# The output gradient's load, the place of the rows' tiles, and the time of b2's sums in a backward kernel

## The chip, the cores and the metric

The program runs on one NeuronCore of a Trainium2 chip. Its engines work beside each other: TensorE (PE in the profile, its weight loads PEld), VectorE (DVE), ScalarE (ACT), GpSimd (POOL) and SyncE (SP), which issues most of the transfers. Each engine works through its own list of instructions in order and waits on semaphores for the others. The metric is the device time of one launch in microseconds (us); lower is better.

## What is computed

One layer, forward and backward, for a sequence of 2048 rows of 512 elements: a spectral filter (FFT over both axes, a product with a complex filter, inverse FFT) and a feed-forward block with a squared ReLU, both modulated by a condition `c`. All gradients are returned.

```python
mod = (_silu(c) @ w_mod).reshape(c.shape[0], 6, 1, -1)
sa, ca, ga, sb, cb, gb = ...
h = _layernorm(x) * (1 + ca) + sa
x = x + ga * irfft2(rfft2(h) * (w_r + 1j * w_i))
h = _layernorm(x) * (1 + cb) + sb
x = x + gb * (relu(h @ w1 + b1) ** 2 @ w2 + b2)
_out, _vjp = jax.vjp(f, A_x, A_w_r, A_w_i, B_w1, B_b1, B_w2, B_b2, c, w_mod)
_grads = _vjp(grad_out)
```

The outputs that matter here: `out_2`, `out_3` (the filter's gradient, w_r and w_i), `out_4`, `out_5` (w1, b1), `out_6`, `out_7` (w2, b2), `out_9` (w_mod), `out_1` (A_x) and `out_8` (c). `grad_out` is the output gradient.

## The kernel before

The function named `tile_adaLN_...` is one long program that a framework orders: tiles are taken from pools, pools lie on two stacks in SBUF (a left one and a right one, `side="right"`), and a pool that is released gives its place to later ones. An instruction that writes a tile waits for all that used the earlier tiles at that place. The framework also draws up each engine's list by priority, and `tc.issue_after(x)` puts what is issued inside it behind x on the same engine. SP's transfers share eight semaphores in turn, so a transfer waits until the eighth before it has landed.

The change lies in the last third, from line 1058 on. What happens there, in order:

- **Spectral stage, backward** (`spec_f23` with `ew_b` and `after_b`, groups gi = 0 to 7). For each group, TensorE makes G (L323, L311), VectorE makes the product Z and the filter's gradient gW from it (`cmul`, L418 to L421), and SP writes gW to `out_2` and `out_3` (L1168). `after_b` fills in TensorE work: products of w1's gradient (`grad_w1`, L1124, sixteen in all; two halves make one tile gw1, which POOL writes, L1130), b1's sums (`grad_b1`, with the tile b4), and four of the six blocks of the modulation's gradient (`gm.emit`, tiles wmc, gmbc, gm_junk and gwm; after groups 0, 1, 3 and 4). It also loads the matrix LG (1.5 MB, after group 4 in the program's text, L1174) and the first two columns hn of the hidden activations, by a transposing load (`load_hn`, L1067).
- **G1** (`spec_g1`, L346 to L367): 128 small matmuls of Z with LG, and casts of their results.
- **Rows stage** (`row_pair`, eight pairs of row tiles): TensorE does psT (L375) and psY (L385); ScalarE and VectorE the layer norm's gradient on two tiles n1 and gxl that SP loads (`load_rows3`, L1216 and L1217). VectorE reads n1 first at L1275. Column sums follow on TensorE (L1256) with a lag of two pairs.
- **w2's gradient** (`grad_w2`, fourteen products of sixteen matmuls, L1196) fills TensorE between the pairs and after them. Each product reads the whole output gradient g_sb (16 tiles of 512 columns, 2 MB) and one hn. VectorE scales the result into gw (L1199), SP writes it (L1200). Products take turns in two PSUM buffers named mm.
- **b2's sums** (`grad_b2`, after the pair t = 10): sixteen matmuls into four quadrants (L1207); `add_quadrants` copies them as b4 (ScalarE, L1097) and the rest as b4l (VectorE, L1098); later, `add` sums the quadrants by two matmuls (L1103), also in a buffer mm, and writes the row. `add` is put on a list that `run_later` empties after the next product of w2's gradient.
- **End**: the other two blocks of the modulation's gradient, the rest of the products, and c's gradient (L1312 to L1320).

The pools in question. Left stack, upwards: gwa (G, gw1 four times, b4), lg2 (LG), spb (Z), f23b (Xb), ewb (p1, p2, gW). Right stack, downwards: lf2 (four spectral matrices LFb), gmp (wmc, gmbc, gm_junk, gwm). After the spectral stage gmp and lf2 are released, and in their place and beyond come gwp (g_sb, hn, gw, b4, b4l, b4r) and below it fin (n1, gxl). g_sb is loaded after the stage's last group (L1219), then the rows of the first two pairs and two more columns hn (L1223).

Of the kernel before, what the change touches and what calls it, by code (L numbers as in the profile page):

```python
# [12 lines left out]
BF16 = mybir.dt.bfloat16  # L13
# [5 lines left out]
D = 512  # L19
# [4 lines left out]
NT = 16  # L24
# [3 lines left out]
P = 128  # L28
# [15 lines left out]
def w_parts(rows, gi):  # L44

    v = rows.rearrange("(q h g) f -> q h g f", h=2, g=16)
    if gi > 0:
        return [(0, 64, v[:, :, gi, :]), (64, 64, v[:, ::-1, 16 - gi, :])]
    c = rows.rearrange("(q c g) f -> q c g f", c=4, g=16)
    return [(0, 64, v[:, :, 0, :]), (64, 32, c[:, 0:2, 8, :]), (96, 32, c[:, 3:1:-1, 8, :])]  # L50
# [15 lines left out]
def build_basic(tc, constp):  # L66
    nc = tc.nc
    K = {}
    ident = constp.tile([P, P], BF16, name="ident")
    make_identity(nc, ident)  # L70
    K["ident"] = ident
    for nm, shape, dt, val in (("ones_sq", [P, P], BF16, 1.0), ("ones_col", [P, 1], BF16, 1.0), ("ones_q", [P, 32], BF16, 0.0), ("onef", [P, 1], FP32, 1.0),
                               ("nhalf", [P, 4], FP32, -0.5), ("npi", [P, 1], FP32, -math.pi), ("eps", [P, 1], FP32, 1e-5)):
        tl = constp.tile(shape, dt, name=nm)
        nc.vector.memset(tl, val)
        K[nm] = tl
    nc.vector.memset(K["ones_q"][:, 0:1], 1.0)
    pid = constp.tile([P, 1], I32, name="pid")
    nc.gpsimd.iota(pid, pattern=[[0, 1]], base=0, channel_multiplier=1)
    K["pid"] = pid  # L80
    pidf = constp.tile([P, 1], FP32, name="pidf")
    nc.vector.tensor_copy(pidf, pid)
    K["pidf"] = pidf
    return K
# [329 lines left out]
def cmul(nc, pool, A, B, outr, outi, conj_a):  # L414

    p1 = pool.tile([P, 2, 2, FP], BF16, name="p1")
    p2 = pool.tile([P, 2, 2, FP], BF16, name="p2")
    nc.vector.tensor_tensor(p1[:, :, :, 0:DF], A[:, :, :, 0:DF], B[:, :, :, 0:DF], op=ALU.mult)  # L418
    nc.vector.tensor_tensor(p2[:, :, :, 0:DF], A[:, :, :, 0:DF], B[:, :, ::-1, 0:DF], op=ALU.mult)
    nc.vector.tensor_tensor(outr, p1[:, :, 0, 0:DF], p1[:, :, 1, 0:DF], op=(ALU.add if conj_a else ALU.subtract))  # L420
    return nc.vector.tensor_tensor(outi, p2[:, :, 0, 0:DF], p2[:, :, 1, 0:DF], op=(ALU.subtract if conj_a else ALU.add)).ins  # L421
# [59 lines left out]
def kernel(  # L481
# [5 lines left out]
    nc = tc.nc  # L487
# [11 lines left out]
    LG_dram = dram.tile([P, 16, 3, P], BF16, name="LG_dram")  # L499

    x_view = A_x.rearrange("b (p t) d -> p (b t) d", t=NT)
    g_view = grad_out.rearrange("b (p t) d -> p (b t) d", t=NT)
# [20 lines left out]
    K = build_basic(tc, constp)  # L523
# [536 lines left out]
    hns, endp = [], {}  # L1060

    def load_hn():
        fc = len(hns)
        if fc < NFC:
            pool = hnp if fc < 2 else endp.get("hn", endp["gw"])
            hns.append(pool.tile([P, NT, P], BF16, name="hn", bufs=2 if pool is not endp.get("hn") else 4))
            nc.sync.dma_start(hns[fc], h_dram[fc, :, :], transpose=True)  # L1067

    lf2 = tc.alloc_tile_pool(name="lf2", bufs=1, side="right")
    gmp = tc.alloc_tile_pool(name="gmp", bufs=1, side="right")  # L1070
    K["LF"] += [lf2.tile([P, 2, 3, P], BF16, name=f"LFb{gi}") for gi in range(4, 8)]
    W4 = 448
    NFB = F // W4
    gwa = tc.alloc_tile_pool(name="gwa", bufs=1)
# [7 lines left out]
    def grad_b1():  # L1082

        ps = mmps.tile([P, SB], FP32, name="mm")
        for t in range(NT):
            for fb in range(NFB):
                nc.tensor.matmul(ps[32 * fb:32 * fb + 32, 0:W4], lhsT=K["ones_q"], rhs=ghn[t // 4][:, t % 4, fb * W4:(fb + 1) * W4],
                                 start=(t == 0), stop=(t == NT - 1), tile_position=(0, 32 * fb))
        b4 = gwa.tile([P, W4], BF16, name="b4", bufs=1)
        nc.scalar.copy(out=b4, in_=ps[:, 0:W4])  # L1090
        nc.gpsimd.dma_start(out_5.rearrange("(q f) -> q f", q=NFB), b4[0:P:32, :])

    def add_quadrants(ps, pool, out, scale=None):
        w = ps.shape[-1]
        b4 = pool.tile([P, w], BF16, name="b4", bufs=1)
        b4l = pool.tile([P, w], BF16, name="b4l", bufs=1)
        nc.scalar.copy(out=b4, in_=ps)  # L1097
        nc.vector.tensor_tensor(b4l, ps, b4, op=ALU.subtract)  # L1098

        def add():  # L1100
            ps = mmps.tile([P, SB], FP32, name="mm")
            for i, x in enumerate((b4, b4l)):
                nc.tensor.matmul(ps[0:1, 0:w], lhsT=K["ones_col"], rhs=x, start=(i == 0), stop=(i == 1))  # L1103
            row = pool.tile([1, w], BF16, name="b4r", bufs=2)
            nc.scalar.copy(out=row, in_=ps[0:1, 0:w])
            if scale is not None:
                nc.vector.tensor_tensor(row, row, scale, op=ALU.mult)
            nc.sync.dma_start(out, row)

        later.append(add)  # L1110

    later = []

    def run_later():
        while later:
            later.pop(0)()

    w1o = {}

    def grad_w1(fb, dc):  # L1120
        fs = slice(fb * W4, (fb + 1) * W4)
        ps = mmps.tile([P, SB], FP32, name="mm")
        for t in range(NT):
            nc.tensor.matmul(ps[:, 0:W4], lhsT=h2_sb[:, t, dc * P:(dc + 1) * P], rhs=ghn[t // 4][:, t % 4, fs],  # L1124
                             start=(t == 0), stop=(t == NT - 1))
        if fb % 2 == 0:
            w1o[0] = gwa.tile([P, 2, W4], BF16, name="gw1", bufs=4)
        nc.scalar.copy(out=w1o[0][:, fb % 2, :], in_=ps[:, 0:W4])
        if fb % 2 == 1:
            nc.gpsimd.dma_start(out4_view[:, dc, (fb - 1) * W4:(fb + 1) * W4], w1o[0].rearrange("p a f -> p (a f)"))  # L1130
# [8 lines left out]
    def fill_w1(n):  # L1139
        for _ in range(n):  # L1140
            if units:
                units.pop(0)()
# [4 lines left out]
    with tc.tile_pool(name="f23b", bufs=2) as fr, tc.tile_pool(name="ewb", bufs=2) as ew:  # L1147
        Xt = {}

        def load(gi):  # L1150
            if gi >= 4:
                nc.sync.dma_start(K["LF"][gi], LF_dram[:, 2 * gi:2 * gi + 2])
            nc.sync.dma_start(Z[gi], wz_dram[:, gi])
            Xt[gi] = fr.tile([P, 2, 2, FP], BF16, name="Xb", bufs=4)
            nc.sync.dma_start(Xt[gi], xs_dram[:, gi])

        for gi in range(4):
            load(gi)
            if gi in (1, 3):
                gm.load(gms[gi // 2][0], gmp)  # L1160

        def ew_b(gi, G):
            cmul(nc, ew, Z[gi], G, Z[gi][:, :, 0, 0:DF], Z[gi][:, :, 1, 0:DF], True)
            gW = ew.tile([P, 2, 2, FP], BF16, name="gW", bufs=3)
            cmul(nc, ew, Xt[gi], G, gW[:, 0, :, 0:DF], gW[:, 1, :, 0:DF], True)
            for i, o in enumerate((out_2, out_3)):
                for p0_, n, rows_ in w_parts(o, gi):
                    K["gW"] = nc.sync.dma_start(rows_, gW[p0_:p0_ + n, i, :, 0:DF]).ins  # L1168

        def after_b(gi):  # L1170
            if gi + 4 < 8:
                load(gi + 4)
            if gi == 4:
                nc.sync.dma_start(K["LG"], LG_dram)  # L1174
            fill_w1(2 if 0 < gi < 6 else 1)
            if gi == 4:
                with tc.issue_after(K["gW"]):
                    load_hn()
                    load_hn()
            if gi in (0, 1, 3, 4):  # L1180
                gms.pop(0)[1]()
                if len(gms) > 1:
                    gm.load(gms[1][0], gmp)

        spec_f23(tc, K, UT, AEs, None, lambda gi: gwa.tile([P, 2, 2, FP], BF16, name="G", bufs=2), ew_b, after_b)
    gmp.release()
    lf2.release()
    gwp = tc.alloc_tile_pool(name="gwp", bufs=1, side="right")
    g_sb = gwp.tile([P, NT, D], BF16, name="g_sb")

    endp["gw"] = gwp

    def grad_w2(fc):
# [13 lines left out]
            nc.tensor.matmul(ps[q:q + 32, :], lhsT=K["ones_q"], rhs=g_sb[:, t, :], start=(t < 4), stop=(t >= 12), tile_position=(0, q))  # L1207
        add_quadrants(ps, gwp, out_7[None, :], modb[0:1, GB_B, :])

    fin = tc.alloc_tile_pool(name="fin", bufs=2, side="right")  # L1210
    rows3 = {}

    def load_rows3(t):
        if t < NT:
            rows3[t] = (fin.tile([P, 2, D], BF16, name="n1"), fin.tile([P, 2, D], BF16, name="gxl"))
            nc.sync.dma_start(rows3[t][0], n1_dram[:, t:t + 2, :])  # L1216
            nc.sync.dma_start(rows3[t][1], gx1_dram[:, t:t + 2, :])  # L1217

    nc.sync.dma_start(g_sb, g_view)  # L1219
    load_rows3(0)  # L1220
    load_rows3(2)
    for _ in range(2):
        load_hn()  # L1223

# [95 lines left out]
        nc.sync.dma_start(out_8.rearrange("b (dc p) -> (b dc) p", p=P), gcr)  # L1320
    psX.release()
    fp.release()
    fin.release()
    gwp.release()
    hnp.release()
    h2p.release()
    cdp.release()
# [36 lines left out]
```

## Time and profile before

Seven runs of the kernel: median 431.56 us, from 428.46 to 432.02. The profiled execution took 429.54 us, with a span of 427.8 us from its first to its last instruction, on one core with a mean granted TensorE clock of 0.996.

| stretch, us | what runs | PE busy | DVE busy | ACT busy | clock | DMA share |
|---|---|---|---|---|---|---|
| 280 to 336.3 | spectral stage, w1's gradient | 55.95 | 44.11 | 33.12 | 1.00 | 0.93 |
| 336.3 to 345.3 | G1 | 8.67 | 7.63 | 4.76 | 1.00 | 0.35 |
| 345.3 to 357 | last of w1's gradient, first pair | 11.68 | 5.02 | 7.69 | 1.00 | 0.85 |
| 357 to 388 | pairs and w2's gradient | 30.59 | 29.32 | 15.47 | 1.00 | 1.10 |
| 388 to 399 | the same, with b2's sums | 7.54 | 9.83 | 4.59 | 0.84 | 1.01 |
| 399 to 412 | last pairs and products | 12.79 | 12.51 | 5.70 | 1.00 | 1.02 |
| 412 to 422.6 | three products, two modulation blocks | 10.52 | 9.69 | 2.84 | 1.00 | 0.51 |
| 422.6 to 427.8 | last writes | 0.22 | 1.10 | 0.00 | 0.99 | 0.22 |

How to read it: the busy time of each engine in each stretch is in us; "clock" is the share of TensorE's full clock that was granted; the DMA share is the mean busy share of the core's 16 DMA engines, as it is inferred from their packets (it can come out above 1).

### The profile page before, as it was taken

Reading aid. Unit: us, or ns where it says so; the run is one execution under the profiler, and the core shown is the slowest. Engines: PE = TensorE matmul, PEld = TensorE weight load, DVE = VectorE, ACT = ScalarE, POOL = GpSimd, SP = SyncE. Lnnn points to the kernel's source line nnn. Section 1 sums busy time; section 2 is a strip of 40 time slices with the busy share of each in tenths; the row PEclk is TensorE's granted clock in tenths of the full one; section 3 lists DMA queues with packets and bytes.
Section 4 is the critical chain, followed back from the end, with each engine's and each line's share of the span. In section 5 each row is a group of like instructions: output and inputs, shape, how many; then the busy total and the mean of one; then the engine's idle time right before and its main releaser. Section 6 shows DMA issues by size and latency. Waiting matters only on the chain.

```text
span 427.8 us, 7115 instructions
## 1 busy us (share of the span) xinstructions
PE 396.3 (93%) x2353; PEld 195.7 (46%) x2375; DVE 354.7 (83%) x862; ACT 256.4 (60%) x487; POOL 54.5 (13%) x135
## 2 busy tenths in 40 slices
PE   2689999999899999999999999999999999996995
PEld 0345446654434443444444444455556655442342
DVE  6889858959995588978897998948997957999995
ACT  4578699778882188148734866464647465537231
POOL 7437940000000000000000000002121000000011
PEclk9999999999999999999999999999999999998999
DMA  8998899969396559767966997979899769999973
GB/s 241 246 268 248 251 234 327 300 231 221 126 355 223 148 95 326 202 156 202 311 170 172 184 318 254 299 199 331 259 281 306 165 208 271 211 265 278 251 203 119
DMA packets 144227, 101.11 MB, mean 236 GB/s; under 512 B 98969, under 2 KB 127518, under 8 KB 143806
## 3 DMA queue, kind: packets, MB, share of 16 engines
q1 hardware_dynamic: 141034, 93.03, 80.7%
q0 software_dynamic: 2592, 7.09, 5.4%
q10 hardware_dynamic: 564, 0.53, 0.4%
q8 instruction: 19, 0.31, 0.3%
q14 instruction: 18, 0.15, 0.1%
HBM read 35.44 MB, written 41.60 MB: 180 GB/s over the span
## 4 chain that ended last, share of the span: by engine, by line
PE 40%; DVE 27%; ACT 16%; DMA 8%; issue 5%; POOL 2%; SPq 1%; ACTq 0%; DVEq 0%; POOLq 0%
PE og L906 10%; PE mm L877 6%; PE mm L712 5%; PE mm L1124 5%; PE mm L1196 5%; DMA n<-n_dram 2%; DMA out_dram<-gwm 2%; ACT gab L717 2%; PE psG L346 2%; ACT AE L329 1%; DMA h_dram<-h 1%; DVE jk L1279 1%; ACT Xs L313 1%; DVE gm_junk L475 1%; ACT AE L330 1%
## 5 line engine op out<-in xcount | busy, mean ns | idle before, releaser
L712 PE MATMUL mm<-gT,w2T 128*128 128x512 bf16 x224 | 57.5, 382 | 3.4 <-ACT gab L717 3.2
L877 PE MATMUL mm<-h2T,w 128*128 128x512 bf16 x224 | 53.4, 379 | 1.5 <-ACT r L879 1.4
L1196 PE MATMUL mm<-g_sb,hn 128*128 128x512 bf16 x217 | 51.7, 388 | 0.7 <-DVE gw L1199 0.2
L906 PE MATMUL og<-w1T,gab 128*128 128x512 bf16 x218 | 49.9, 379 | 1.0 <-DVE o L971 0.7
L1124 PE MATMUL mm<-gab,h_sb 128*128 128x448 bf16 x256 | 50.7, 352 | 0.0
L906 PE MATMUL og<-w,h 128*128 128x512 bf16 x217 | 49.1, 379 | 0.3
L879 ACT ACTIVATE r<-mm,b1col 128x512 bf16<-128x512 f32 x56 | 37.0, 686 | 6.1 <-PE mm L877 3.3
L877 PEld LDWEIGHTS <-w 128*128 128x128 bf16 x224 | 21.1, 97 | 30.0 <-issue 8.3
L1124 PEld LDWEIGHTS <-h_sb 128*128 128x128 bf16 x256 | 24.6, 98 | 21.8 <-issue 0.6
L1196 PEld LDWEIGHTS <-hn 128*128 128x128 bf16 x224 | 21.6, 100 | 27.0 <-issue 4.5
L906 PEld LDWEIGHTS <-h 128*128 128x128 bf16 x224 | 21.8, 98 | 26.1 <-issue 1.0
L906 PEld LDWEIGHTS <-gab 128*128 128x128 bf16 x224 | 21.6, 98 | 25.9 <-issue 1.4
L712 PEld LDWEIGHTS <-w2T 128*128 128x128 bf16 x224 | 21.2, 98 | 22.8 <-issue 6.8
L919 ACT CAST G<-og 128x512 bf16<-128x512 f32 x16 | 9.2, 580 | 28.1 <-PE og L906 28.1
L1274 ACT ACTIVATE gs<-gn,inv 128x512 bf16<-128x512 bf16 x16 | 11.4, 716 | 23.6 <-DVE gn L1272 23.6
L295 POOL MEMSET AE<- 128x2 bf16 x4 | 0.3, 102 | 193.7 <-PE mm L877 193.7
L477 POOL DMA_DIRECT2D out_dram<-gwm x12 | 8.8, 731 | 116.5 <-DVE gwm L474 60.9
L881 DVE TENSOR_TENSOR h<-r 128x1024 bf16<-128x1024 bf16 x28 | 19.2, 686 | 4.8 <-ACT r L879 4.8
L717 ACT CAST gab<-mm 128x512 bf16<-128x512 f32 x36 | 21.3, 600 | 1.7 <-PE mm L712 1.5
L475 DVE SCALAR_TENSOR_TENSOR gm_junk<-wmc,onef,gmbc 128x512 bf16<-128x512 bf16 x24 | 17.9, 748 | 4.2 <-ACT gmbc L465 2.3
L715 DVE CAST gab<-mm 128x512 bf16<-128x512 f32 x20 | 13.8, 688 | 7.0 <-PE mm L712 6.8
L377 ACT ACTIVATE Tsb<-psT 128x512 bf16<-128x512 f32 x32 | 18.4, 606 | 1.5 <-PE psT L375 1.5
(290 smaller groups left out, 798.6 us busy)
## 6 DMA issues: line engine op xcount, KB each, us to landing
h_dram<-h SPq DMA_DIRECT2D x28, 256.0 KB, 3.3
gh_dram<-gab SPq DMA_DIRECT2D x28, 256.0 KB, 3.8
w<-in_B_w_dram SPq DMA_DIRECT2D x2, 1792.0 KB
wmc<-in_w_mod_dram SPq DMA_DIRECT2D x12, 256.0 KB, 5.2
out_dram<-gwm POOLq DMA_DIRECT2D x12, 256.0 KB, 4.9
wz_dram<-Z SPq DMA_DIRECT2D x8, 258.0 KB, 4.0
xs_dram<-Xs SPq DMA_DIRECT2D x8, 258.0 KB, 4.1
Z<-wz_dram SPq DMA_DIRECT2D x8, 258.0 KB, 4.8
```

What stands on the lines that cost most here:

```text
L377: nc.scalar.activation(Tsb, ps, AF.Copy, scale=EF_S)
L475: nc.vector.scalar_tensor_tensor(out=junk, in0=wmc[:, i, :], scalar=K["onef"], in1=gmbc, op0=ALU.mult, op1=ALU.mult, accum_out=self.gsc[:, ...
L712: nc.tensor.matmul(ps, lhsT=w2T[:, dc, fc * P:(fc + 1) * P], rhs=gT[b][:, :, dc, :], start=(dc == 0), stop=(dc == 3))
L715: nc.vector.tensor_copy(out=gaT[b][:, fc, :], in_=ps)
L717: nc.scalar.copy(out=gaT[b][:, fc, :], in_=ps)
L877: nc.tensor.matmul(ps, lhsT=w1[:, dc, (fc + i) * P:(fc + i + 1) * P], rhs=h2T[b][:, :, dc, :], start=(dc == 0), stop=(dc == 3))
L879: nc.scalar.activation(r[:, i, :], ps, AF.Relu, bias=b1col[:, fc + i:fc + i + 1])
L881: nc.vector.tensor_tensor(h2, r, r, op=ALU.mult)
L906: nc.tensor.matmul(ps, lhsT=lhs(fc), rhs=rhs[:, fc, :], start=(fc == 0), stop=(fc == NFC - 1))
L1124: nc.tensor.matmul(ps[:, 0:W4], lhsT=h2_sb[:, t, dc * P:(dc + 1) * P], rhs=ghn[t // 4][:, t % 4, fs], start=(t == 0), stop=(t == NT - 1))
L1196: nc.tensor.matmul(ps, lhsT=hns[fc][:, t, :], rhs=g_sb[:, t, :], start=(t == 0), stop=(t == NT - 1))
L1274: nc.scalar.activation(gs[:, i, :], gn[:, i, :], AF.Copy, scale=inv1[:, t + i:t + i + 1], accum_out=rr[:, i, 0:1])
```

## The change

g_sb gets a pool of its own, gsp, on the right stack in the place of gmp, which is released at group 5; its load is issued there, behind group 5's writes of gW. For this, b1's tile b4 moves from gwa to gmp, and gw1 has three buffers instead of four. lf2 stays to the end. fin is allocated right after gsp, ahead of gwp, and the loads of the first two pairs of rows are put behind the load of g_sb. LG's load moves from group 4 to group 3 in the text, behind group 3's writes of gW. The list `later` holds a counter with each entry, and `add` runs when four products of w2's gradient have been issued after it was put there, instead of one.

```diff
-        b4 = gwa.tile([P, W4], BF16, name="b4", bufs=1)
+        b4 = gmp.tile([P, W4], BF16, name="b4", bufs=1)
...
-        later.append(add)
+        later.append([4, add])
 
     later = []
 
-    def run_later():
-        while later:
-            later.pop(0)()
+    def run_later(n=1):
+        if later:
+            later[0][0] -= n
+            if later[0][0] <= 0:
+                later.pop(0)[1]()
...
-            w1o[0] = gwa.tile([P, 2, W4], BF16, name="gw1", bufs=4)
+            w1o[0] = gwa.tile([P, 2, W4], BF16, name="gw1", bufs=3)
...
-            if gi == 4:
-                nc.sync.dma_start(K["LG"], LG_dram)
+            if gi == 3:
+                with tc.issue_after(K["gW"]):
+                    nc.sync.dma_start(K["LG"], LG_dram)
             fill_w1(2 if 0 < gi < 6 else 1)
             if gi == 4:
                 with tc.issue_after(K["gW"]):
                     load_hn()
                     load_hn()
+            if gi == 5:
+                gmp.release()
+                endp["g"] = tc.alloc_tile_pool(name="gsp", bufs=1, side="right")
+                endp["g_sb"] = endp["g"].tile([P, NT, D], BF16, name="g_sb")
+                with tc.issue_after(K["gW"]):
+                    K["g_load"] = nc.sync.dma_start(endp["g_sb"], g_view).ins
...
-    gmp.release()
-    lf2.release()
+    g_sb = endp["g_sb"]
+    fin = tc.alloc_tile_pool(name="fin", bufs=2, side="right")
     gwp = tc.alloc_tile_pool(name="gwp", bufs=1, side="right")
-    g_sb = gwp.tile([P, NT, D], BF16, name="g_sb")
...
-    fin = tc.alloc_tile_pool(name="fin", bufs=2, side="right")
...
-    nc.sync.dma_start(g_sb, g_view)
-    load_rows3(0)
-    load_rows3(2)
+    with tc.issue_after(K["g_load"]):
+        load_rows3(0)
+        load_rows3(2)
     for _ in range(2):
         load_hn()
...
     fp.release()
+    gwp.release()
     fin.release()
-    gwp.release()
+    endp["g"].release()
+    lf2.release()
```

## The prediction

> **What bounds the kernel now.** I read the page's head first, then the chain of waits from 340 us on, the list of waits, the busy time by stretches around the places that the chain names, and the timeline of SP's queue. From the page:
>
> ```profile
> span 427.8 us, 7115 instructions
> PE 396.3 (93%) x2353; PEld 195.7 (46%) x2375; DVE 354.7 (83%) x862; ACT 256.4 (60%) x487; POOL 54.5 (13%) x135
> ```
>
> TensorE is busy in 93% of the span, so an edit pays only where TensorE stands still or runs slowly, or where VectorE makes it do so later. The chain (start, us, what) shows the two places in the last 85 us:
>
> ```profile
> 346.32 9.31 DMA n<-n_dram
> 355.65 0.69 DVE q L1275
> ...
> 392.10 0.61 DVE b4l L1098
> 392.75 0.38 PE mm L1103
> ...
> 393.75 5.09 PE mm L1196 x16
> ```
>
> First, VectorE stands until the rows' tile n1 has landed, 9.3 us after its issue; from there the chain runs on VectorE until 392. Second, TensorE waits for b4l, the low half of b2's sums, which VectorE reaches late. The list of waits prices both, and SP's:
>
> ```profile
> PE mm L1103 <- DVE b4l L1098: 2.8, 1, 2.8
> DVE q L1275 <- DMA n<-n_dram: 2.3, 1, 2.3
> ...
> DVE gw L1199 <- PE mm L1196: 1.2, 2, 0.8
> ...
> PE mm L1103 <- ACT b L1097: 0.7, 1, 0.7
> ...
> SPq L1219 <- DMA out_dram<-gW: 2.9, 3, 2.6
> ```
>
> By stretches (length; busy time and count of PE, PEld, DVE, ACT, POOL; then granted clock, DMA share, GB/s), round the second place and over the whole stretch that VectorE leads:
>
> ```profile
> 322.00:339.00 17.00, 17.00 (x120) 10.39 (x118) 14.76 (x35) 9.67 (x18) 2.56 (x4) 1.00 0.94 250
> 389.60:392.70 3.10, 0.37 (x2) 0.08 (x2) 3.10 (x7) 0.82 (x3) 0.00 (x0) 1.00 0.90 245
> 392.70:396.20 3.50, 3.45 (x19) 1.54 (x19) 3.09 (x10) 3.09 (x7) 0.00 (x0) 0.62 1.12 269
> 353.40:423.70 70.30, 65.25 (x348) 28.36 (x353) 63.72 (x155) 31.19 (x69) 3.44 (x5) 0.98 0.97 240
> ```
>
> After the standstill the granted clock is 0.62: the next product takes 5.09 us. The last row says that both engines are nearly full to the end (VectorE 63.7 of 70.3 us), so neither can be helped alone. SP's queue (start, us that the issue held the queue, line):
>
> ```profile
> 333.94 8.63 SPq L1168 DMA_DIRECT2D out_dram<-gW  x12
> 345.91 0.35 SPq L1219 DMA_DIRECT2D g_sb<-in_grad_out_dram  x1
> 346.32 0.42 SPq L1216 DMA_DIRECT2D n<-n_dram  x1
> ...
> 348.44 12.55 SPq L1067 DMA_TRANSPOSE hn<-h_dram  x2
> ```
>
> The 2 MB of g_sb are held until the last filter gradient has left its tile (the wait of 2.9 us above), and the rows' tiles queue behind them. Between 343 and 346 us nothing moves on the DMA engines.
>
> **Part 1: the output gradient at group 5.** g_sb (16,384 B per partition) gets gmp's place: 14,336 B plus 896 for b4, so 1,152 B hang over. The left side is shorter by one gw1 and b4, 1,792 + 896 = 2,688 B; by the addresses of the kernel before (top of ewb 147,344, bottom of gmp 155,520) the overhang and the 8,192 B of fin then lie free of gW. What g_sb waits for is gmp's last use: the write of gwm for group 4, issued by POOL at 326.17, median 4.9 us to land, so about 331. It stands behind the four issues of gW of group 5, a third of the twelve above: 333.94 + 8.63/3 = 336.8 us. Before, g_sb and four row loads, 3 MB, had landed 9.8 us after 345.9, about 0.31 MB per us. The same five from 336.8 (at worst with the 0.5 MB of two gW between them, 1.7 us, and SP's issues of 0.6 us each, eight, 4.9 us) land between 346.6 and 353.2. VectorE needs n1 when gn of L1272 ends, at 353.4. So the 2.3 us go: **VectorE starts its rows 2.3 us earlier**; bounds 1.5 (if they land late) and 2.3. The next pair's gs is there at 357.85 us, and VectorE would ask for it at 360.23 - 2.26 = 357.97, so the gain is not lost one pair later. Delayed in turn are gW of groups 6 and 7, behind 2 MB: by up to 6.5 us. Nothing reads them; the tiles of gwp that come over their place (hn of columns 2 and 3, gw) wait for them. SP is held there until about 348 instead of 345.8, with these two transposes behind; their products run at 365 and 370 us, the loads land 13 us after the issue at the slowest, 361. Cost nothing; if that cover went, 1 to 2 us.
>
> **Part 2: LG behind group 3's gradients.** LG (1.5 MB) leaves SP's place at 315.60 and comes after the four issues of 3.28 us, about 319. In front, Xb and gW of group 3 move up by 0.4 us. TensorE wants LG at 336.5; even at the 9.3 us that the far larger crowd above took it lands by 329. Written out earlier, the blocks gwm of group 3 come free sooner: ScalarE and VectorE waited 1.9 and 1.7 us for them in 322 to 326. That saves TensorE nothing, because it is busy 17.00 of 17.00 us in that stretch. I take 0; bounds -0.3 (the one wait of TensorE for a cast, at 339.5) and +7 (the slower rival).
>
> **Part 3: b4 and gw1.** No instruction is added. Three buffers of gw1 instead of four: each is filled by two products of 3.1 us, so the third last was sent 12 us before, and its landing takes 6.2. Nothing; if one came late, ScalarE would stand for the rest of it and TensorE one product later. lf2 kept to the end and the release orders issue nothing.
>
> **Part 4: the sums of b2 four products later.** The two matmuls of L1103, ScalarE's copy (0.57 us), VectorE's scaling (0.41) and SP's issue (0.31) stay, behind four products instead of one, some 14 us after b4l's inputs. Gone from TensorE are 2.8 + 0.7 = 3.5 us of waiting, and the slow clock: 5.09 us against 3.51 (three products in 10.53 us at 412.04) is 1.6. Behind the waiting matmul stood the colsums, psT and the product, on which VectorE's next rows hang. What is late next: the sum takes one of the two buffers mm at its new place, so the product after it must wait for gw of the product just before. Nearest rows: between 0 (gw at once while psum frees) and 1.4 (one VectorE operation of 0.69 and gw's 0.68); I take 0.7, since gw has high priority. TensorE: 3.5 + 1.6 - 0.7 = **4.4 us**.
>
> A rule of the Trainium skill bears on the 1.6. "TensorE: Matmul & The Clock Gate", Part 1: The HAM clock gate, has the clock halved after an idle window of about 3.4 us, in windows that run free. The row shows 0.62 after only 3.1 us, with 0.37 busy in them. Taken strictly the rule speaks against this part: such a gap need not cool the clock, the 1.6 would be chance, and the sum would be 2.8 us for this part. I follow the row.
>
> **The sum.** VectorE has to keep up: it gains 2.3 from the rows, the 1.2 that its gw waited for TensorE and the 0.4 that its scaling waited for a copy in the cold stretch (394.4), and half of the remaining idle time that I can't assign by name, 0.3: 4.2 us. The end hangs on the smaller of 4.4 and 4.2. The tail behind the last product (gw, its transfer, 5.2 us) stays. The profiled execution takes 429.54 us with its span of 427.8: 425.3 after. The median of the runs shown is 431.56, 2.0 above that execution; the same 4.2 less gives 427.4 us.
>
> **Rivals.**
> *VectorE doesn't yield.* It is busy 63.7 of 70.3 us; if TensorE, once free at 389, only runs into the next buffer whose gw is not done, the 3.5 us come back in pieces and only the clock's 1.6 or less is kept: 430.0. For it: TensorE's waits at 378 and 388 are VectorE's lateness. Against it: gw of the product before (386.28) is through when the next product would start, at 389.5, and so is the following one (392.6, less 2.3).
> *More than the sum.* TensorE's whole idle time from 357 to 422.6 goes, about 4.2 us, with the cold 1.6, and the last blocks move up with it: -6.2, so 425.4. Against it: b4's buffer and VectorE's 63.7 us of work.
> *LG late: slower.* If LG is placed in SP's queue behind the two transposes that hold it from 327.5 to 333.9, 1.5 MB land 5 us (at 0.31 MB per us) and 2 us of start later, at 341 to 342. TensorE, at G1 since 336.5, stands 5 us, and the clock falls by the row above, 1.6 to 2. Against that stand the 4.2: 431.56 + 7 - 4.2 = 434.4. It decides from the moment LG lands after 336.5; up to there nothing is lost. For it: each transposing load holds SP 2 to 9 us. Against it: LG comes earlier in the program than those loads.
> *The rows don't move.* If the row loads still stand behind gW of group 7, they land after 353: part 1 is 0 and the sum about 2.5, 429.0; it lies in my range.
>
> **How the numbers follow.** Forecast 427.4 with 0.63 (own range 425.9 to 429.2); more than the sum 0.10; VectorE doesn't yield 0.13; LG late 0.14. A measurement here tells about 0.5%, 2.2 us, from no change: faster below 429.4. Of the forecast, nearly all lies there: faster 0.72, same 0.14, slower 0.14. The range leaves out the slower case and a little of the best: 424.9 to 431.0.
>
> **What would show it.** g_sb issued near 337 and n1 landed before 353; no wait of L1275 for n; no TensorE wait of over 1.5 us at L1103, which now follows the tenth product; a granted clock of 1.00 from 388 to 400; LG landed before TensorE's first L346. I am wrong if TensorE stands at L346, if L1275 still waits for its rows, or if the time of the waits for b4l turns up at L1196 behind gw.

## The result, and the profile after

The changed kernel takes 427.72 us (median of 23 runs, 425.97 to 430.19) against 430.95 us for the kernel before beside it (58 runs). The ratio is 0.9939, 95% interval 0.9924 to 0.9955: 0.61% faster, about 2.6 us. (The two medians by themselves lie 3.2 us apart; gains below go by the ratio.) The forecast was 427.4 us, with a gain of 4.2; so the direction is right and the gain is smaller. That the time itself came within 0.3 us is in part luck: the forecast started from a median of 431.56, which by the ratio would have become 428.9. The profiled execution took 427.19 us (before 429.54). In these two traces the whole changed part of the kernel lies 0.66 us earlier already ahead of its first changed instruction (first psB of L323 at 281.13 instead of 281.79), so 0.66 of the 2.4 us between the spans is no work of the change. Issue and landing times below are as the traces have them; where two kernels are set side by side, such a shift has to be taken off.

The page's head:

```profile
span 425.4 us, 7116 instructions
...
PE 395.0 (93%) x2353; PEld 195.3 (46%) x2375; DVE 354.9 (83%) x862; ACT 256.3 (60%) x487; POOL 55.0 (13%) x135
```

The changed text has other line numbers: n is now L1222 (before L1216), q L1281 (L1275), the products of w2's gradient L1203 (L1196), gw L1206 (L1199), the column sums L1262 (L1256), LG L1177, the gradients gW L1170, g_sb L1188. The chain of waits (start, us, what) still goes through the rows' tile:

```profile
338.84 9.51 DMA out_dram<-gW
348.36 5.98 DMA n<-n_dram
354.37 0.69 DVE q L1281
```

The list of waits of the same stretch, TensorE's and VectorE's:

```profile
DVE q L1281 <- DMA n<-n_dram: 1.5, 1, 1.5
PE psY L385 <- ACT Tsb L377: 1.4, 1, 1.4
...
PE acc L1262 <- DVE gh L270: 1.2, 1, 1.2
...
PE mm L1203 <- DVE gw L1206: 0.4, 1, 0.4
...
DVE gw L1206 <- PE mm L1203: 0.4, 1, 0.4
PE acc L1262 <- DVE q L1281: 0.3, 1, 0.3
```

Three things are to be seen. The waits at L1103 (2.8 and 0.7 us before) are gone. TensorE stands in four other places instead, 1.4 + 1.2 + 0.4 + 0.3 = 3.3 us, each time for something that hangs on VectorE. And VectorE still stands for its rows, 1.5 us instead of 2.3. By stretches (length; busy time and count of PE, PEld, DVE, ACT, POOL; granted clock, DMA share, GB/s):

```profile
387.00:398.00 11.00, 9.41 (x52) 3.90 (x51) 10.87 (x26) 4.29 (x10) 0.00 (x0) 1.00 1.04 218
...
352.90:421.00 68.10, 63.49 (x348) 28.00 (x353) 63.46 (x156) 31.22 (x69) 3.45 (x5) 1.00 0.98 241
```

The clock is whole where b2's sums stood before. The stretch that VectorE leads is 68.1 us instead of 70.3, with about the same VectorE work (63.5 against 63.7). SP's queue (start, us that the issue held it, line):

```profile
319.20 0.59 SPq L1177 DMA_DIRECT2D LGb<-LG_dram  x1
...
338.35 0.40 SPq L1188 DMA_DIRECT2D g_sb<-in_grad_out_dram  x1
338.84 9.07 SPq L1170 DMA_DIRECT2D out_dram<-gW  x8
348.36 0.33 SPq L1222 DMA_DIRECT2D n<-n_dram  x1
```

g_sb goes out 7.6 us sooner than before (6.9 with the shift of 0.66 us taken off). But n is issued at 348.36, 2.0 us later than before (346.32; 2.7 with the shift taken off): the framework put all eight writes of gW of groups 6 and 7 between g_sb and n. Those eight now share the DMA engines with g_sb's 2 MB and land a median 10.0 us after their issue (3.6 before), one of their issues is held 2.7 us until g_sb itself has landed, and the row loads take their turn among SP's eight semaphores behind them (SP waits 0.6 us at L1222 and 3.0 us at L1223 for such a write). From the list of SP's waits:

```profile
SPq L1223 <- DMA out_dram<-gW: 3.0, 2, 1.8
...
SPq L1170 <- DMA g_sb<-in_grad_out_dram: 2.7, 1, 2.7
```

No tile makes n wait for gW any more; only the place in the queue does.

### The profile page after: what moved, and what is told of

It is laid out like the page before. It is cut to its first block, busy times and chain, and to the rows that moved or that the text cites. A ratio compares the mean times of both kernels' runs of the same rounds, so it can differ in the third digit from the quotient of the medians.

```text
span 425.4 us, 7116 instructions
## 1 busy us (share of the span) xinstructions
PE 395.0 (93%) x2353; PEld 195.3 (46%) x2375; DVE 354.9 (83%) x862; ACT 256.3 (60%) x487; POOL 55.0 (13%) x135
## 4 chain that ended last, share of the span: by engine, by line
PE 45%; DVE 22%; ACT 16%; DMA 9%; issue 4%; POOL 2%; ACTq 0%; DVEq 0%; POOLq 0%
PE og L906 12%; PE mm L877 10%; PE mm L712 5%; PE mm L1126 5%; PE mm L1203 3%; DMA out_dram<-gW 2%; DMA out_dram<-gwm 2%; DMA n<-n_dram 2%; ACT gab L717 2%; DVE jk L1285 2%; PE psG L346 2%; ACT AE L329 1%; ACT Xs L313 1%; DMA out_dram<-gx 1%; ACT AE L330 1%
## 5 line engine op out<-in xcount | busy, mean ns | idle before, releaser
L1203 PE MATMUL mm<-g_sb,hn 128*128 128x512 bf16 x217 | 49.8, 379 | 0.9 <-DVE gw L1206 0.4
L1203 PEld LDWEIGHTS <-hn 128*128 128x128 bf16 x224 | 21.2, 98 | 27.3 <-issue 3.6
L715 DVE CAST gab<-mm 128x512 bf16<-128x512 f32 x20 | 13.7, 687 | 7.1 <-PE mm L712 6.9
```

The source lines that it names most:

```text
L715: nc.vector.tensor_copy(out=gaT[b][:, fc, :], in_=ps)
L1203: nc.tensor.matmul(ps, lhsT=hns[fc][:, t, :], rhs=g_sb[:, t, :], start=(t == 0), stop=(t == NT - 1))
```

## The experiments

The theory V: from the first rows to the last product VectorE sets the pace, so what TensorE gets back counts only as far as VectorE's own waits shrink. The rival T: TensorE sets it, and each us of its standstill that goes is a us won.

**Part 4 alone.** The kernel before with only the counter on `later`:

```diff
-        later.append(add)
+        later.append([4, add])
```

> The kernel before with one part of the change alone: b2's sums four products later. Theory V (VectorE sets the end of the rows stage, TensorE's standstill is given back): VectorE had only 1.2 + 0.4 us of idle time there, so 1 to 2 us less than before, about 429.5 us against 431, and new TensorE waits of 2 us or more on VectorE or on ScalarE behind it. Theory T (the sum of the prediction: TensorE sets the end): the whole 4.4 us, about 426.5. Both expect no wait of over 1.5 us at the sums' matmuls and a granted clock of 1.00 from 388 to 400 us.

Measured: 430.24 us, ratio 0.9984 (0.9966 to 1.0003). Its waits:

```profile
DVE q L1277 <- DMA n<-n_dram: 3.0, 1, 3.0
...
PE psY L385 <- ACT Tsb L377: 1.9, 1, 1.9
...
PE acc L1258 <- DVE gh L270: 1.2, 1, 1.2
...
PE mm L1198 <- DVE gw L1201: 1.0, 3, 0.4
...
PE acc L1258 <- DVE q L1277: 0.3, 1, 0.3
```

The standstill of 3.5 us comes back as 1.9 + 1.2 + 1.0 + 0.3 = 4.4 us, and the granted clock is 1.00 throughout. So 5.1 us of standstill and slow clock on TensorE, taken away by themselves, gain 0.7 us with an interval that reaches to nothing.

**Parts 1 to 3 alone.** The changed kernel with `later.append([1, add])`:

> The changed kernel with the sums one product later, as before: the loads' part alone. The standstill of 3 us and the slow clock after it should be back. Theory V: VectorE starts its rows some 0.7 us earlier and TensorE's wait for b4l ends with VectorE, so 0.5 to 1.3 us less than before, about 430. Theory T: the standstill costs its full 4.4 us, VectorE's earlier start is lost in it: within 0.5 us of before, 431.

Measured: 430.13 us, ratio 0.9979 (0.9950 to 1.0009). From its list of waits, and by stretches:

```profile
PE mm L1103 <- DVE b4l L1098: 2.8, 1, 2.8
DVE gw L1206 <- PE mm L1203: 2.3, 2, 1.9
...
DVE q L1281 <- DMA n<-n_dram: 1.6, 1, 1.6
```

```profile
388.00:392.00 4.00, 1.22 (x8) 0.26 (x7) 4.00 (x9) 1.22 (x3) 0.00 (x0) 0.81 0.99 232
392.00:396.00 4.00, 4.00 (x19) 1.91 (x19) 3.88 (x12) 2.69 (x7) 0.00 (x0) 0.50 1.00 261
```

Here VectorE does start sooner, and loses it at 390 to 400: it waits 2.3 us for products that run behind the standstill at half clock. Both halves of the change have small gains whose intervals touch 1; their sum, 0.37%, and the whole, 0.61%, can't be told apart by these medians. That the two need each other is read from the waits, not from the medians.

The traces say it more sharply. For each kernel I take the stretch from 16.8 us after the start of G1 (where VectorE asks for n1 in the kernel before) to the end of the last product, and take off VectorE's waits for n, for a product (mm) or for gs at L266:

| kernel | stretch, us | VectorE's waits in it | rest |
|---|---|---|---|
| before | 69.24 | 2.3 + 1.2 | 65.7 |
| part 4 alone | 69.15 | 3.0 + 0.4 | 65.8 |
| parts 1 to 3 alone | 69.59 | 1.6 + 2.3 | 65.7 |
| changed | 67.54 | 1.5 | 66.0 |
| changed, second trace | 66.93 | 1.1 | 65.8 |
| rows first (below) | 67.20 | 1.3 | 65.9 |
| LG back (below) | 66.17 | 0 | 66.2 |
| rows by GpSimd (below) | 66.13 | 0 | 66.1 |

The stretch varies by 3.5 us over these eight traces, which do the same work, and the rest by 0.5. That VectorE has no other long waits makes the last column even; what counts is which waits make up the third. In the second row TensorE's standstill is gone, and the stretch stays because n came later there (3.0 us of waiting instead of 2.3; why it came later is not shown) and VectorE waited 0.4 us at L266. From the fourth row on TensorE does the same in the same order, only the wait for n differs, and the stretch follows it nearly us for us. The gain of the change is the fall from 3.5 to 1.5 or 1.1.

**Less work for TensorE.** The changed kernel with the column sums of six of the eight pairs left out:

```diff
-            late.add(lambda: colsums1(t, gh1, q1))
+            if t in (0, NT - 2):
+                late.add(lambda: colsums1(t, gh1, q1))
```

> The changed kernel with less for TensorE: the column sums of six of the eight pairs of rows are left out (24 matmuls, about 0.33 us for four side by side, 2.0 us in all), and with them the two waits at the sums, 1.2 and 0.3 us. Theory V: VectorE does as much as before, so 0 to 1 us less than the changed kernel, about 427.3. Theory T: 2 to 3.5 us less, about 424.8.

Measured: 427.63 us, ratio 0.9929 (0.9900 to 0.9957), the same as the change. Its TensorE waits more instead:

```profile
PE mm L1203 <- DVE gw L1206: 1.8, 1, 1.8
...
PE psY L385 <- ACT Tsb L377: 1.7, 1, 1.7
PE mm L1324 <- DVE gcb L1322: 1.6, 1, 1.6
```

By the medians this is nearer to V, though the interval reaches down to 0.9900, 1.7 us below the change. The trace says that TensorE's work counts in part. Its front is late without any work of the edit (first psB at 283.58, 281.13 and 282.64 in the two traces of the changed kernel), so it is counted from the start of G1: the last product ends after 81.75 us, against 84.34 and 83.73, and what follows that product takes 5.82 us instead of 5.19, with the wait of the last line above in it. That leaves the end 1.4 to 2.0 us sooner, and only 0.6 to 1.0 of this is VectorE's shorter wait for n (0.5 us). Nor does this run keep to the table's last column: its stretch is 64.95 us, less the 0.5 of waiting 64.4, though VectorE has the same work; 0.7 us of that work now lies behind the last product. So the run speaks against T in its full form, in which 2.0 us less work is 2.0 us less time, but some 0.8 to 1.0 us of the 2.0 do count in this trace, and the table's constancy holds only for kernels that leave TensorE its work.

**Less work for VectorE, first try.** gxl's addition left out of `out_1` (L1292 reads gn and gs only):

> The changed kernel with one VectorE operation less in each pair of rows: the add of the first part of the gradient, gxl, into out_1 is left out (8 operations of 0.60 us apart, 4.8 us in all); its loads stay. Theory V (after the change VectorE paces the rows stage, and TensorE's waits for it, 3.4 us from 388 to 406, are its lateness): these waits go and 2 to 3.4 us with them, about 425 us; no more, since TensorE's own work then sets the end. Theory T (TensorE's work sets the end): 0 to 1 us less.

Measured: 436.25 us, ratio 1.0118 (1.0087 to 1.0149). Inconclusive for V: with gxl unread, six of its loads went out together, ahead of n, and VectorE waited 13.7 us for n in three places. It does show what late rows cost. One of TensorE's waits there was of 2.05 us, and the product behind it, which takes 3.62 us in the changed kernel's timeline, took 5.25:

```profile
376.10 5.25 PE L1203 MATMUL mm<-g_sb,hn 128*128 128x512 bf16 x16 [2.05 <-DVE gw L1206]
```

**The same with gxl read**, beside an unchanged copy of the changed kernel:

```diff
-            nc.vector.tensor_tensor(gs, gn, gs, op=ALU.add)
             gx = fp.tile([P, 2, D], BF16, name="gx")
-            nc.vector.tensor_tensor(gx, gs, gxl, op=ALU.add)
+            nc.vector.tensor_tensor(gx, gn, gxl, op=ALU.add)
```

> The changed kernel as it is, as the measure for the two beside it: 427.7 us, ratio to the kernel before 0.992 to 0.996, by every theory. If it lies outside of that, the two others are read against this run and not against the earlier ones.

> The changed kernel in which gx is made of gn and gxl alone: the addition of gs to gn is left out, so out_1 lacks that part. gxl is still read, so the order of the loads stays. VectorE has eight operations of 0.60 us less, 4.8 us, of which some 4.2 us lie before the end of the products. V (VectorE paces the row pairs): the waits of the products for gw go and the end comes 2 to 3.4 us sooner than in the changed kernel, 424.3 to 425.7 us, bounded by TensorE's own waits of 3.4 us behind G1. T (TensorE alone paces it): 0 to 1 us, 426.7 to 427.7 us.

Measured: the unchanged copy 429.05 us, ratio 0.9946 (0.9921 to 0.9972), which is the result once more; the other 430.06 us, ratio 0.9997 (0.9965 to 1.0028). Neither V nor T said so: less VectorE work made it slower. Its waits, SP's queue and TensorE:

```profile
DVE q L1281 <- DMA n<-n_dram: 6.7, 3, 3.4
...
PE acc L1262 <- DVE gh L270: 3.6, 1, 3.6
...
PE acc L1262 <- DVE q L1281: 2.0, 1, 2.0
```

```profile
393.95 1.95 SPq L1067 DMA_TRANSPOSE hn<-h_dram  x1
396.01 0.51 SPq L1292 DMA_DIRECT2D out_dram<-gx  x1
396.58 0.42 SPq L1222 DMA_DIRECT2D n<-n_dram  x1
```

VectorE is ready for the next pair at 397.4, but its n, the seventh, was issued at 396.58 only, behind the tenth transposing load, and lands at 400.2. In the changed kernel the seventh n stands behind the tenth transposing load too, but both go out sooner:

```profile
387.87 4.04 SPq L1067 DMA_TRANSPOSE hn<-h_dram  x1
392.34 0.34 SPq L1207 DMA_DIRECT2D out_dram<-gw  x1
392.79 0.37 SPq L1222 DMA_DIRECT2D n<-n_dram  x1
```

The ninth load is what moved: it goes out at 381.66 in the changed kernel, ahead of a pair's gx and gxl, and at 387.40 here, behind them. The framework drew up SP's list in another order when one VectorE operation was missing. TensorE then stands 2.0 and 3.6 us and the clock is 0.50 from 404 to 408 (this execution took 432.87 us, 2.8 above the median of its kernel, so the trace shows the matter larger than it mostly is). So there is a third pace close behind VectorE's, the row loads in SP's queue, which V as I stated it lacks.

**Both less.** The two last edits together:

> The same with the column sums of six of the eight row pairs left out too (2.0 us of TensorE; part of the sums that go into the modulation gradient is missing). V with room on both sides: the two savings add, 2.0 us below the kernel with the addition left out alone, about 422.3 to 423.7 us. T: the whole 2.0 us comes from TensorE and it ends at 424.7 to 425.7 us, though the column sums alone gave nothing. If neither the addition nor the sums nor both move the end, the pace is set by something outside of both, the loads of n or the end of the kernel.

Measured: 426.07 us, ratio 0.9882 (0.9844 to 0.9921): 0.64% below the unchanged copy, 2.8 us. That is short of the 4 us or more that V expected and within the 2.0 to 3.0 us that T did. Its trace has 3.5 us of waits for n and this one:

```profile
393.71 1.07 PE L385 MATMUL psY<-Tsb,TAT 128*128 128x512 bf16 x2 [3.18 <-ACT Tsb L377]
394.58 4.99 PE L1203 MATMUL mm<-g_sb,hn 128*128 128x512 bf16 x16
```

How much of these 2.8 us belongs to which saving is left open, since SP's order moved with the edits; so V is not confirmed by it, and T's number is not proof of T.

**The rows ahead of g_sb.** fin is allocated at group 5 and the loads of the first two pairs are issued before g_sb's:

> The changed kernel with the rows' first four loads issued at group 5 too, ahead of the output gradient's load, so that neither 2 MB nor the eight writes of gW of groups 6 and 7 stand before them. Both theories: n1 lands before 346 us and VectorE's wait for it (1.5 us in the changed kernel) is gone. Theory V: VectorE starts 1.5 us earlier and the end moves with it, 1 to 1.5 us less than the changed kernel, about 426.4. Theory T: TensorE's products set the end, 0 to 0.4 us less, about 427.5.

Measured: 428.49 us, ratio 0.9947 (0.9917 to 0.9976): the same as the change. SP's queue:

```profile
339.06 0.59 SPq L1152 DMA_DIRECT2D n<-n_dram  x1
...
341.34 0.33 SPq L1200 DMA_DIRECT2D g_sb<-in_grad_out_dram  x1
341.96 10.07 SPq L1179 DMA_DIRECT2D out_dram<-gW  x8
356.42 4.85 SPq L1067 DMA_TRANSPOSE hn<-h_dram  x2
361.32 0.58 SPq L1152 DMA_DIRECT2D n<-n_dram  x1
```

The first n no longer makes VectorE wait, but SP stands for gW until 356, and the later row loads do not go out sooner: counted from the first psB, the fifth pair's n is issued at 97.0 us (96.4 and 95.6 in the two traces of the changed kernel), while VectorE, which started earlier, asks for it earlier and waits:

```profile
384.75 0.69 DVE L1282 TENSOR_TENSOR q<-gh,n 128x1024 bf16<-128x1024 bf16 x1 [1.06 <-DMA n<-n_dram]
```

The wait has moved on.

**The rows by GpSimd's queue.** Both loads of `load_rows3` as `nc.gpsimd.dma_start`:

> The changed kernel in which the sixteen loads of n and gxl are issued from GpSimd's queue and not from SP's; the order of TensorE's, VectorE's and ScalarE's instructions stays as it is, and so does all work. It asks what the row loads' places in SP's queue cost, behind the writes of gW at first and behind the transposes of hn later. L (the row loads are a third pace of the stage beside VectorE and TensorE): the first n lies there before the first q, VectorE waits for no n, the first q starts 0.5 us (bounded by gh) sooner, SP gets to the transposes of hn sooner, and the end comes 0.5 to 1.5 us sooner than in the changed kernel, ratio 0.990 to 0.993. V alone (only VectorE paces it, the loads are hidden but for 0.5 us): within 0.5 us of the changed kernel. G (GpSimd writes descriptors while VectorE runs, as its arithmetic held VectorE's operations up before): VectorE's operations beside an issue lengthen, 430 us or more.

Measured: 435.66 us, ratio 1.0124 (1.0086 to 1.0162), slower, and not for the reason given beside G: VectorE's operations are no longer (q 683 ns, 685 in the changed kernel). GpSimd's queue, and TensorE's only long wait ahead of G1:

```profile
288.27 0.60 POOL L1222 DMA_DIRECT2D n<-n_dram  x1 [35.10 <-PE psC L311]
288.86 0.57 POOL L1223 DMA_DIRECT2D gxl<-gx_dram  x1
```

```profile
PE mm L1126 <- ACT gmbc L465: 4.1, 1, 4.1
```

The first row loads went out at 288, as soon as their place was free and some 70 us before they are read. Their 1 MB now goes out beside the loads of Z and Xb, wmc lands late (VectorE waits 7.1 us for it, 1.0 in the changed kernel), and G1 starts 60.46 us after the first psB instead of 54.74. Behind G1 the kernel does what L says: no wait for n, and the stretch is 66.13 us instead of 67.54 and 66.93. So rows in time are worth another 0.8 to 1.4 us, which this form pays for fivefold in front. Only the later pairs on that queue, with the first two left with SP, was not tried.

**LG back at group 4** in the changed kernel:

> The changed kernel with LG's load at group 4 in the text and bound to nothing, as before. In this kernel's list it then stands ahead of the first Z, near 284 us, not at 315 as before, since its new place in memory is free earlier. If LG's part of the change is worth nothing (the prediction): within 0.5 us of the changed kernel. If it is what keeps 1.5 MB out of the way of the first Z and Xb: VectorE's first products come 4 to 5 us later, and since TensorE has 3 us products of w1's gradient to fill in, 0 to 3 us longer than the changed kernel.

Measured: 431.38 us, ratio 0.9989 (0.9957 to 1.0021), so 0.5% or 2.1 us worse than the change. SP's queue and the waits:

```profile
284.97 0.43 SPq L1176 DMA_DIRECT2D LGb<-LG_dram  x1
288.15 0.32 SPq L1155 DMA_DIRECT2D Z<-wz_dram  x1
```

```profile
DVE p L418 <- DMA Z<-wz_dram: 5.9, 1, 5.9
...
PE mm L1126 <- ACT gmbc L465: 1.9, 1, 1.9
```

In the new layout the place of LG is free early, and without `issue_after` the framework hoists its 1.5 MB ahead of the first Z. VectorE waits for Z, and G1 starts 2.07 us later.

**q on GpSimd**, in the changed kernel and in the one with the rows first (L1281 as `nc.gpsimd.tensor_tensor`):

> The changed kernel with the product q (L1281, needed by the column sums two pairs later alone) on GpSimd, which stands idle from 357 to 412 us: 8 operations of 0.60 us go from VectorE. Theory V: as with one operation left out, 2 to 3 us less, about 425, if the operation takes GpSimd less than a pair's 6.9 us and VectorE's operations beside it keep their times. If the two engines hinder each other, VectorE's operations beside it lengthen and it is no gain or a loss, 427 to 431. Theory T: 0 to 1 us less.

> The rows' loads ahead of the output gradient's and q on GpSimd, together. Theory V: VectorE starts 1.5 us earlier and has 4.8 us less to do, so TensorE sets the end: 3 to 4 us less than the changed kernel, about 424. If GpSimd hinders VectorE: no better than the changed kernel. Theory T: 0 to 1 us less.

Measured: 438.42 us, ratio 1.0169 (1.0130 to 1.0208), and 436.03 us, ratio 1.0115 (1.0079 to 1.0151). In the first of them:

```profile
356.00 2.49 POOL L1281 TENSOR_TENSOR q<-gh,n 128x1024 bf16<-128x1024 bf16 x1 [3.86 <-DMA gxl<-gx_dram]
...
356.61 2.42 DVE L1285 SCALAR_TENSOR_TENSOR jk<-gs,onef,n 128x512 bf16<-128x512 bf16 x1
```

GpSimd takes 2.5 us for q, and VectorE's jk beside it 2.42 us instead of 0.75. What was taken off VectorE came back as longer operations there. This doesn't speak on V.

## Why the prediction was right, and where its size was off

- **What sets the end.** "The end hangs on the smaller of 4.4 and 4.2", with VectorE's the smaller, agrees with the runs in the main: TensorE's side alone gains 0.7 us, if anything (part 4 alone), and 2.0 us less of its work hardly moves the median. But VectorE is not the only one. When it has less to do, the row loads in SP's queue come next at once (less VectorE work), and in the trace with less TensorE work, as perhaps in the run with less of both, a part of TensorE's saving counts beside it. "The smaller of the two" is a bound that these runs come near to, not a law.
- **Part 1 is the term that was mis-sized.** I had the rows land between 346.6 and 353.2 and took the whole gain, 2.3 us, though the late end left only 0.2 us to the 353.4 at which VectorE needs n1. n1 landed at 354.3, and VectorE's wait fell from 2.3 to 1.5 (1.1 in the second trace): 0.8 to 1.2 us. The step that failed is the landing time. g_sb went out at 338.35 and not at 336.8, because the two transposing loads ahead of it held SP until 335.2 and not until 333.9. And "at worst with two gW between them" was no worst case but what happened: the eight writes of groups 6 and 7, which that bound had at 4.9 us of SP's time, held SP for 9.07, of which 2.7 were a wait for g_sb itself that the sum had at nothing. From g_sb's issue to n1's landing it was 16.0 us; the early bound had 9.8 for it and the late one 16.4. (The 9.8 us for 3 MB are misread: by that time before, 355.6, only the first n had landed, and the second landed at 357.5, 11.5 us after 345.9.) This is the rival "the rows don't move" in its cause, though not in full, because g_sb's transfer starts earlier. That rival's gain as written, 2.5, is nearer to the measured 2.6 than the forecast, but it is not what its terms give: without the 2.3 they are 1.2 + 0.4 + 0.3 = 1.9, so 429.7 us.
- **Part 4, TensorE.** 3.5 us of waiting and the slow clock went as expected: no wait at L1103 after the tenth product, the product behind that place takes 3.62 us in the timeline, where it took 5.29 before (5.09 in the chain). The new wait of 0.7 us for a PSUM buffer is 0.4 us. But 3.3 us of other waits came in, at psY, the column sums and gw. The warning sign that I named, waits for b4l turning up at L1196 behind gw, looked at one of the four places only.
- **Part 4, VectorE.** The 1.2 us that gw waited for a product went (0.4 us is left, outside of the stretch measured here): right. The wait of 0.4 us for the copy is gone from the list as well, but neither it nor the 0.3 us of idle time without a name shows in the time: the rest of the stretch is 65.7 us before and 66.0 and 65.8 after.
- **The sum as measured**: VectorE's waits fall from 3.5 to 1.5 or 1.1, 2.0 to 2.4 us; the stretch is 1.7 to 2.3 us shorter; the medians give 2.6, interval 1.9 to 3.3. Forecast were 4.2.
- **The clock.** I followed the row and not the strict reading of the rule. In these runs waits of TensorE of up to 1.9 us left the clock at 1.00 (part 4 alone), and single waits of 2.05 (less VectorE, first try), 2.5 (q on GpSimd), 2.8 (parts 1 to 3 alone), 3.2 (both less) and 3.6 us (less VectorE with gxl read) were each followed by a slow product or a stretch near 0.50, as were two waits of 1.7 and 1.9 us that lay 0.7 us apart (q on GpSimd). So the slow clock belonged to the standstill. But as the end hung on VectorE, the 1.6 us entered the time only through the products that VectorE waited for.
- **Part 2** is 0 against the kernel before: LG landed 10.3 us after its issue, at 329.5, 6.4 us ahead of G1, and G1 starts 54.74 us after the first psB in both kernels. The rival "LG late" didn't occur. The work it does in the new layout, 2.1 us, I had not seen: it holds LG back from 285 us.
- **Part 3** is 0: nothing ahead of G1 moved.
- **"VectorE doesn't yield"** was nearer than its chance of 0.13 says: its mechanism ran in full (3.3 us came back in pieces), and the gain came from VectorE's own waits instead. "More than the sum" is out.

## What to carry to other kernels

Where two engines are both nine tenths full, as here, a standstill of one is worth little more than what it saves the other in waits: list the waits of the engine that leads, and predict from these first. Then look for what comes next when they are gone, here the row loads in SP's queue. When a load is moved, write down the whole list of its queue after the move, with the writes that fall between and the time that these will need beside the moved bytes. An early place can be too early: a load whose tile comes free sooner is hoisted past the loads that are needed first (LG and the rows by GpSimd each cost 2 to 6 us that way).

## What the runs showed of the hardware

- A GpSimd tensor operation of 2.49 us on bf16 tiles in SBUF stretched a VectorE operation beside it from 0.75 to 2.42 us, while GpSimd's issuing of DMAs (0.54 us each) left VectorE's at 683 ns. The Trainium skill, "SBUF — State Buffer", Who interferes with whom, has VectorE and GpSimd sharing one pair of ports that one instruction holds to its end; the first of these rows agrees.
- With 2 MB of g_sb on the way, eight 64 KB writes issued behind it landed after a median 10.0 us instead of 3.6.
